# Gradient stores of a decode attention block: each 1.5 MB dV and dK tile stored in two halves

## The chip, the cores and the metric

The kernel runs on one core of a Trainium2 chip. The time is the device time of one execution, in microseconds. Each version is timed in several runs; one further execution is recorded by the profiler, and all durations by line, engine or stretch come from that one. Engines are named as in the profile: PE multiplies matrices, PEld loads its weights, DVE works on whole tiles elementwise, ACT does copies and functions, POOL and SP here do hardly more than start DMA transfers. The core has 16 DMA engines, which all queues share.

## What is computed

A block with a modulated layernorm, attention over a cache for one token, and an MLP, and then its gradients. The part that matters here is the attention and the gradients of its caches:

```python
B, Sq, D = (1, 1, 640)
Hq, Hkv, Sk, Dh = (32, 32, 8192, 192)
...
scores = jnp.einsum('bhqd,bhkd->bhqk', q, k) * Dh ** (-0.5)
p = _softmax(scores, axis=-1)
o = jnp.einsum('bhqk,bhkd->bhqd', p, v)
...
_out, _vjp = jax.vjp(_f, A_x, A_k_cache, A_v_cache, A_wq, A_wo, B_w3, B_w4, c, w_mod)
_grads = _vjp(grad_out)
```

K and V are 32 heads of 8192 x 192 in bf16, 3.1 MB each per head. Both are read, V twice (for the output and again for dP = dO V), and dK and dV of the same size are written. With p the softmax row of a head, dV is the outer product of p and dO, and dK the outer product of dS = p (dP - c) and q.

## The kernel before

**Two stages.** The first, up to about 560 us, goes through the heads with loads of K and V and computes the output. Then come a short seam, which does the MLP and its gradients, and the second stage, lines 1420 to 1507, which computes dK, dV and the gradients of the weights. It is a loop over 64 steps `s`; a step is one half `t` of the cache rows of one head (4096 rows), in the order of `ht(s)`, from the last head to the first. The order on PE, DVE, ACT and SP is the order in the program; POOL's DMAs go out in program order too.

**The layout.** A tile of a step has 128 partitions of 32 rows of 192 values: 12288 bytes per partition, 1.5 MB (1536 KB) in all. Row `j` of partition `p` lies beside row `j + 1` in memory, so a whole tile is a run of 12288 bytes for each partition. `JH` is 32 rows, a tile; `JQ` is 16 rows, half a tile.

**A step.** `dot_sum` and line 1427 turn the dot products of V and dO into `dS4`. Then these are woven into each other:
- `dv(0)` to `dv(7)` (lines 1113 to 1123) make dV in eight groups: four matmuls into PSUM (line 1122) and one ACT copy into the tile (line 1123) each. `gs` says which group comes when. An even group number writes rows 0 to 15 of every partition, the first half of the tile, an odd one rows 16 to 31.
- `dk_part` (line 1127) makes dK on DVE in two halves, `0:JQ` and `JQ:JH`.
- `tree_q` (line 1111), `mul_q` (line 1092) and `half_q` compute the dot products of the next steps, in halves too.
- `slot()` puts in a share of the side work: transposes and sums for the weights' gradients, their loads through SP, and their stores of 0.48 or 0.96 MB through POOL (lines 1217 and 1244).
- `load_v` asks SP for the V tile of step s + 5 once its buffer is free.

**The stores.** `dv_store` (line 1377) and `dk_store` (line 1381) take a range of rows. `dv_store` goes through POOL unless another queue is given. For most steps there is one `dk_store` of the whole tile after the second `dk_part`, and one `dv_store` of the whole tile after `dv(7)`. Exceptions: at step 0, dV was made before the loop and dK is stored in halves; at step 63 both are stored in halves, dV through SP, with `gs` in the order 0, 2, 4, 6, 1, 3, 5, 7.

**The buffers.** `OL` gives dV and dK of a step one of five tiles in turn (`OB`, named KB, VB and `qs_bc` in the profile). So dK of step s is written where dV of step s - 2 was, and dV of step s where dK of step s - 3 was; the new write waits until the store of those rows has landed. A wait concerns the rows that are written. V tiles have four other buffers, which come free when both `mul_q` of a step are done.

**POOL's DMA semaphores.** The framework gives the DMAs that POOL starts eight semaphores in turn. Ahead of each of these DMAs stands a semaphore instruction on POOL, which waits for the landing of the DMA eight before it on POOL; the wait for the data follows with the DMA itself.

Of the kernel before, what the change touches and what calls it, by code (L numbers as in the profile page):

```python
# [20 lines left out]
def kernel(  # L21
# [26 lines left out]
    nc = tc.nc  # L48
# [7 lines left out]
    JH = J // 2  # L56
    JQ = J // 4
# [59 lines left out]
    def tcol(n, name, dtype=FP32):  # L117
        return tmp.tile([P, n], dtype, name=name)
# [208 lines left out]
    def load_v(h, t, v):  # L327
        nc.sync.dma_start(out=v, in_=V_hd[h][:, t * JH : (t + 1) * JH, :])
        return v
# [16 lines left out]
    def dot_sum(ps, dst):  # L346
        V_.reduce_sum(out=dst, in_=ps, axis=AX.X)  # L347
# [11 lines left out]
    NS = 2 * HQ  # L359

    def load_er(s, eng=nc.scalar, er=None):

        if er is None:
            er = bst.tile([P, R8, P], BF16, name="er_b", bufs=2)
        h, t = ht(s)
        r0 = h * J + t * JH
        eng.dma_start(out=er[0:P:32, :, :].rearrange("r k p -> r (k p)"), in_=eT_d[r0 : r0 + JH, :].rearrange("(r k) p -> r (k p)", r=4))
        return er

    def ht(s):  # L370

        return H1 - s // 2, (1 - s % 2 if s < 2 else s % 2)
# [668 lines left out]
    def do_of(h):  # L1041
        return do_r[:, (TL - h // 2) % NDR, (h % 2) * DH : (h % 2 + 1) * DH]
# [24 lines left out]
    def q_bc(h, pool=psB, tag="b"):  # L1067
        ps = pool.tile([P, 2 * P], FP32, name="q_ps", tag=tag)
        T_.matmul(ps[:, 0:DH], lhsT=pick(HQ, h), rhs=q_rows, start=True, stop=True)
        qh = bst.tile([P, DH], BF16, name="qh", bufs=2)  # L1070
        A_.copy(out=qh, in_=ps[:, 0:DH])
        return qh
# [18 lines left out]
    def mul_q(s, q):  # L1091
        V_.tensor_tensor(  # L1092
            out=pq[:, q],
            in0=v_l[s][:, q * JQ : (q + 1) * JQ, :],
            in1=do_of(ht(s)[0])[:, None, :].to_broadcast([P, JQ, DH]),
            op=ALU.mult,
        )
# [4 lines left out]
    def half_q(s, q):  # L1102
        if halved(s, q):
            V_.tensor_tensor(out=pq[:, q, :, 0:HW], in0=pq[:, q, :, 0:HW], in1=pq[:, q, :, HW:DH], op=ALU.add)

    def tree_q(ps, s, q, lo=0, hi=DH // TS):
        w = DH
        if halved(s, q):
            w, lo, hi = HW, (lo + 1) // 2, (hi + 1) // 2
        for k in range(lo * TS, hi * TS, TS):  # L1110
            T_.matmul(ps[:, q * JQ : (q + 1) * JQ, :], lhsT=ident_bf, rhs=pq[:, q, :, k : k + TS], start=(k == 0), stop=(k == w - TS), skip_group_check=True)  # L1111

    def dv_groups(dV, er, doh, gs):

        dV4 = dV.rearrange("p (r k) d -> p r (k d)", r=4)
        for g in gs:
            m, q = divmod(g, 2)
            ps = psV.tile([P, 2, 512], FP32, name="dv_ps", tag="v")
            for k in range(2):
                for b in range(2):  # L1120
                    p0 = 32 * (2 * q + b)
                    T_.matmul(ps[:, b, k * DH : (k + 1) * DH], lhsT=er[p0 : p0 + 1, 2 * m + k, :], rhs=doh[p0 : p0 + 1, :], start=True, stop=True)  # L1122
            A_.copy(out=dV4[:, 2 * q : 2 * q + 2, m * PW : (m + 1) * PW], in_=ps[:, :, 0:PW])  # L1123

    def dk_part(dK, qh, dS4, lo, hi):
        n = hi - lo
        V_.tensor_tensor(  # L1127
            out=dK[:, lo:hi, :].rearrange("p j (a b) -> p j a b", b=4),
            in0=qh.rearrange("p (a b) -> p a b", b=4)[:, None, :, :].to_broadcast([P, n, DH // 4, 4]),
            in1=dS4[:, lo:hi, None, :].to_broadcast([P, n, DH // 4, 4]),  # L1130
            op=ALU.mult,
        )
# [207 lines left out]
    def slot():  # L1340
        prog[0] += 1
        k = prog[0] - 1
        due = sum(n for i, n in RAMP.items() if i <= k) if k < R0 else NR + -(-(NP - NR) * (k - R0 + 1) // (SLOTS - R0))
        while prog[1] < min(due, NP):
            next(side)
            prog[1] += 1

    def v_buf(s):
        return KY if s == 0 else VB[2] if s == 1 else (VB[0], VB[1], KX, KY)[(s - 2) % 4]
# [8 lines left out]
    def dq_rows(t, kb, dS4):  # L1358

        ps = psB.tile([P, 512], FP32, name="dq_ps", tag="b")  # L1360
        for j in range(JH):
            p0 = 32 * (j % 4)
            T_.matmul(ps[p0 : p0 + 32, 0:DH], lhsT=dS4[:, j, 0:1].to_broadcast([P, 32]), rhs=kb[:, j, :], start=(j < 4), stop=(j >= JH - 4), skip_group_check=True)
        row = bst.tile([P, DH], FP32, name="dq_junk")
        A_.copy(out=row, in_=ps[:, 0:DH])
        return row

    def dq_cols(row):
        cp = psS.tile([P, 4], FP32, name="dq_c", tag="s")
        T_.matmul(cp[:, 0:1], lhsT=row[:, 0:P], rhs=c32[:, 0:1], start=True, stop=True)  # L1370
        T_.matmul(cp[64:128, 1:2], lhsT=row[:, P:DH], rhs=c32[:, 0:1], start=True, stop=True)
        V_.tensor_tensor(out=dq_x[:, 2:3], in0=cp[:, 0:1], in1=dq_x[:, 2:3], op=ALU.add)
        V_.tensor_tensor(out=dq_x[64:128, 1:2], in0=cp[64:128, 1:2], in1=dq_x[64:128, 1:2], op=ALU.add)

    def dv_store(s, dV, lo, hi, eng=nc.gpsimd):
        h, t = ht(s)
        eng.dma_start(out=dV_hd[h][:, t * JH + lo : t * JH + hi, :], in_=dV[:, lo:hi, :])  # L1377

    def dk_store(s, dK, lo, hi):
        h, t = ht(s)  # L1380
        nc.gpsimd.dma_start(out=dK_hd[h][:, t * JH + lo : t * JH + hi, :], in_=dK[:, lo:hi, :])  # L1381
# [38 lines left out]
    for s in range(NS):  # L1420
        h, t = ht(s)
        nxt = s + 1 < NS
        doh = do_of(h)
        dP = tcol(JH, "dP")
        dot_sum(ps, dP)
        dS4 = bst.tile([P, JH, 4], BF16, name="dS4", bufs=2)
        V_.scalar_tensor_tensor(
            out=dS4,
            in0=dP[:, :, None].to_broadcast([P, JH, 4]),
            scalar=cpr[:, h : h + 1],  # L1430
            in1=E_all[:, h, t * JH : (t + 1) * JH, None].to_broadcast([P, JH, 4]),
            op0=ALU.subtract,
            op1=ALU.mult,
        )
        dV, dK = OL[2 * s], OL[2 * s + 1]
        gs = [0, 1, 2, 3, 4, 5, 6, 7]
        if not nxt:
            gs = [0, 2, 4, 6, 1, 3, 5, 7]
        if s == 0:
            gs = [None] * 8  # L1440
        else:
            er = er_l.pop(s)
        if nxt:
            ps = psR.tile([P, JH, TS], FP32, name="dot_ps")

        def dv(k):
            if gs[k] is not None:
                dv_groups(dV, er, doh, (gs[k],))

        def tree(q, lo, hi):  # L1450
            if nxt:
                tree_q(ps, s + 1, q, lo, hi)

        dv(0)
        dv(1)
        slot()
        tree(0, 0, 4)
        if nxt:
            mul_q(s + 1, 1)
            half_q(s + 1, 1)  # L1460
            v_l.pop(s + 1, None)
        if 0 < s < NS - 5:
            v_l[s + 5] = load_v(*ht(s + 5), v_buf(s + 5))
        dv(2)
        tree(0, 4, 8)
        dv(3)
        tree(0, 8, 12)
        dk_part(dK, qh, dS4, 0, JQ)
        if not nxt:
            dv_store(s, dV, 0, JQ, nc.sync)  # L1470
        if s in (0, NS - 1):
            dk_store(s, dK, 0, JQ)
        slot()
        dv(4)
        tree(1, 0, 3)
        dk_part(dK, qh, dS4, JQ, JH)
        if s > 0 and late0:
            late0.pop(0)()
        dk_store(s, dK, JQ if s in (0, NS - 1) else 0, JH)
        if row is not None:  # L1480
            dq_cols(row)
            row = None
        dv(5)
        tree(1, 3, 6)
        slot()
        dv(6)
        tree(1, 6, 9)
        dv(7)
        if s + 2 < NS:
            er_l[s + 2] = load_er(s + 2)  # L1490
        if s == 0:
            pass
        elif nxt:
            dv_store(s, dV, 0, JH)
        else:
            dv_store(s, dV, JQ, JH, nc.sync)
        tree(1, 9, 12)
        if h == H1:
            row = dq_rows(t, (KD, KE)[t], dS4)
        if s + 2 < NS:  # L1500
            assert (s + 2) // 4 in done
            mul_q(s + 2, 0)
            half_q(s + 2, 0)
        if nxt and ht(s + 1)[0] != h:
            qh = q_bc(ht(s + 1)[0])
        done_s[0] = s + 1
        slot()
# [33 lines left out]
```

## Time and profile before

| What | Value |
| --- | --- |
| Median of 3 runs | 1391.87 us (1390.95 to 1393.46) |
| The profiled execution's own time | 1394.3 us |
| Its span, first to last instruction | 1392.5 us |
| PE / DVE / ACT / POOL busy | 1181.5 / 1110.0 / 912.3 / 108.3 us |
| DMA packets and bytes | 76872, 569.38 MB, mean 409 GB/s |
| Of the packets, under 8 KB | 37182 |
| Whole dV and dK stores on POOL (1536 KB) | 74 + 25 + 25 |
| Halves on POOL (768 KB) from the dV and dK buffers | 4 + 2 |
| Halves on SP at step 63 | 2 |
| PE clock granted, from 640 us on | 0.50 to 0.57 |

All stretches are microseconds from the span's start. A line of the profile's groups names the line of the kernel, the engine, the operation and the tiles (written <- read). A wait line reads: engine, tile and line that waited, what released it, total us, times, the longest. A timeline row is start, duration, engine, line, operation, tiles, and in brackets the idle time of the engine before it with what ended it; a DMA row is the issue on the engine's queue, not the transfer. The DMA share of a stretch is the time of the packets that start in it over the time of 16 engines.

### The profile page before, as it was taken

The page shows a single profiled execution, that of the slowest core. Times are in us where ns is not written, and L with a number is a line of the kernel's source. Part 1 is how long each engine was busy: PE and PEld are TensorE (multiplying, and loading weights), DVE is VectorE, ACT ScalarE, POOL GpSimd, SP SyncE. Part 2 cuts the span into 40 slices and gives each one's busy share as a digit, 9 for nine tenths or more (in the row PEclk, how much of TensorE's full clock was granted, in tenths as well). Part 3 has the DMA queues.
Part 4 walks back from the last instruction along what each step waited for, and adds up shares of the span by engine and source line. Part 5 has one row for each costly group of instructions (what it writes and reads, how often), then busy time and mean ns, then how long its engine had stood idle before and what let it go on. Part 6 is the DMA issues. An engine that isn't in the chain of part 4 may idle for free.

```text
span 1392.5 us, 30504 instructions
## 1 busy us (share of the span) xinstructions
PE 1181.5 (85%) x12712; PEld 743.2 (53%) x12712; DVE 1110.0 (80%) x1455; ACT 912.3 (66%) x2007; POOL 108.3 (8%) x196
## 2 busy tenths in 40 slices
PE   3888999999899999988767998788989699779985
PEld 2777777778787778633323443334444344334431
DVE  4999999999999999986764875776766767768775
ACT  0677777777777778866554766665656566556664
POOL 0000000000000000111110110111110101101110
PEclk7899999999999999765555555665555555555555
DMA  9999999999999999699999999999999999999998
GB/s 381 390 404 422 413 424 424 410 417 420 418 420 419 408 418 387 231 419 427 423 397 401 428 424 427 423 425 425 426 418 425 421 409 427 420 409 384 423 412 353
DMA packets 76872, 569.38 MB, mean 409 GB/s; under 512 B 7422, under 2 KB 25198, under 8 KB 37182
## 3 DMA queue, kind: packets, MB, share of 16 engines
q1 hardware_dynamic: 51594, 342.03, 60.2%
q0 software_dynamic: 24624, 224.89, 38.5%
q8 instruction: 99, 1.62, 0.4%
q10 hardware_dynamic: 516, 0.51, 0.1%
q14 instruction: 39, 0.32, 0.1%
HBM read 340.97 MB, written 226.44 MB: 407 GB/s over the span
## 4 chain that ended last, share of the span: by engine, by line
issue 39%; DVE 23%; DMA 18%; PE 12%; POOL 4%; ACT 3%; POOLq 0%; SPq 0%; ACTq 0%; DVEq 0%
DMA KB<-in_A_k_cache_dram 10%; DVE prod L333 10%; DVE prod L337 5%; DVE vs L403 3%; DMA out_dram<-KB 3%; PE mp L425 2%; DMA out_dram<-VB 2%; PE dot_ps L1111 2%; PE half_ps L343 2%; POOL out_dram L1381 2%; DMA stg<-in_A_wq_dram 2%; POOL out_dram L1377 2%; PE mp L430 1%; DMA out_dram<-qs_bc 1%; PE dv_ps L1122 1%
## 5 line engine op out<-in xcount | busy, mean ns | idle before, releaser
L1111 PE MATMUL dot_ps<-pq,ident_bf 128*128 128x256 bf16 x1494 | 377.7, 396 | 21.7 <-DVE dP L347 19.8
L410 ACT ACTIVATE vs<-VB,Ef 128x192 bf16<-128x192 bf16 x840 | 303.6, 447 | 0.0
L1123 ACT CAST KB<-dv_ps 128x768 bf16<-128x768 f32 x312 | 241.4, 805 | 77.8 <-PE dv_ps L1122 76.5
L1111 PEld LDWEIGHTS <-ident_bf 128*128 128x128 bf16 x1494 | 149.9, 123 | 175.0 <-issue 136.2
L1122 PE MATMUL dv_ps<-do_r,er_b 1*128 1x192 bf16 x2016 | 226.8, 335 | 4.3 <-ACT KB L1123 3.1
L333 DVE TENSOR_TENSOR prod<-KB,qs_bc 128x6144 bf16<-128x6144 bf16 x62 | 207.9, 3353 | 25.4 <-DMA KB<-in_A_k_cache_dram 21.7
L425 PE MATMUL mp<-vs,KB 128*128 128x193 bf16 x1984 | 189.5, 247 | 4.4 <-ACT vs L410 3.3
L425 PEld LDWEIGHTS <-KB 128*128 128x128 bf16 x1984 | 168.9, 98 | 13.7 <-issue 7.6
L1127 DVE TENSOR_TENSOR KB<-qh,dS 128x3072 bf16<-128x3072 bf16 x74 | 127.7, 1752 | 54.8 <-DMA out_dram<-KB 40.7
L904 ACT COPY wT<-wT_ps 128x1024 bf16<-128x1024 bf16 x82 | 79.1, 965 | 119.3 <-PE wT_ps L903 119.2
L1122 PEld LDWEIGHTS <-er_b 1*128 1x128 bf16 x2016 | 69.3, 104 | 145.7 <-issue 143.8
L343 PE MATMUL half_ps<-prod,ident_bf 128*128 128x256 bf16 x744 | 95.1, 279 | 43.7 <-DVE prod L337 43.6
L403 DVE TENSOR_TENSOR vs<-VB,E 128x1728 bf16<-128x1728 bf16 x120 | 123.6, 1051 | 0.3 <-ACT vs L410 0.3
L1092 DVE TENSOR_TENSOR pq<-VB,do_r 128x3072 bf16<-128x3072 bf16 x66 | 115.4, 1749 | 9.7 <-PE dot_ps L1111 9.7
L1092 DVE TENSOR_TENSOR pq<-KB,do_r 128x3072 bf16<-128x3072 bf16 x62 | 108.4, 1749 | 6.4 <-PE dot_ps L1111 6.4
L337 DVE TENSOR_TENSOR prod<-prod 128x3072 bf16<-128x3072 bf16 x62 | 108.7, 1753 | 1.0
L343 PEld LDWEIGHTS <-ident_bf 128*128 128x128 bf16 x744 | 72.9, 100 | 62.2 <-issue 53.2
L430 PE MATMUL mp<-vs,KB 128*64 128x193 bf16 x1968 | 106.0, 250 | 0.0
L1123 ACT CAST VB<-dv_ps 128x768 bf16<-128x768 f32 x96 | 75.2, 803 | 39.7 <-PE dv_ps L1122 39.6
L347 DVE TENSOR_REDUCE dP<-dot_ps 128x32 f32<-128x512 f32 x64 | 44.0, 687 | 68.7 <-PE dot_ps L1111 68.5
L1123 ACT CAST qs_bc<-dv_ps 128x768 bf16<-128x768 f32 x104 | 79.9, 805 | 21.2 <-PE dv_ps L1122 20.8
L390 ACT ACTIVATE E<-S_h,negm 128x256 bf16<-128x256 f32 x31 | 15.8, 508 | 114.6 <-DVE negm L561 112.3
(377 smaller groups left out, 1256.8 us busy)
## 6 DMA issues: line engine op xcount, KB each, us to landing
VB<-in_A_v_cache_dram SPq DMA_DIRECT2D x93, 1536.0 KB
out_dram<-KB POOLq DMA_DIRECT2D x74, 1536.0 KB, 15.7
KB<-in_A_k_cache_dram SPq DMA_DIRECT2D x63, 1536.0 KB
KB<-in_A_v_cache_dram SPq DMA_DIRECT2D x29, 1536.0 KB
out_dram<-qs_bc POOLq DMA_DIRECT2D x25, 1536.0 KB, 15.2
out_dram<-VB POOLq DMA_DIRECT2D x25, 1536.0 KB, 15.0
wo_st<-in_A_wo_dram SPq DMA_DIRECT2D x31, 480.0 KB
w_st<-in_A_wq_dram SPq DMA_DIRECT2D x12, 960.0 KB
```

Of the source, the lines that this page charges most:

```text
L333: V_.tensor_tensor(out=prod, in0=src, in1=vec[:, None, :].to_broadcast([P, JH, DH]), op=ALU.mult)
L337: V_.tensor_tensor(out=prod[:, :, 0:HW], in0=prod[:, :, 0:HW], in1=prod[:, :, DH - HW : DH], op=ALU.add)
L343: T_.matmul(ps, lhsT=ident_bf, rhs=prod[:, :, k : k + TF], start=(k == 0), stop=(k == w - TF))
L403: V_.tensor_tensor(out=vs[:, 0:n, 0:DH].rearrange("p j (a b) -> p j a b", b=4), in0=v[:, v0 : v0 + n, :].rearrange("p j (a b) -> p j a b", ...
L410: A_.activation(out=vs[:, k, 0:DH], in_=v[:, v0 + k, :], func=ACT.Copy, scale=Ef[:, j0 + k : j0 + k + 1])
L425: T_.matmul(mp[:, 0:MW], lhsT=kb[:, j0 + k, 0:P], rhs=vs[:, k, 0:MW], start=(q == 0 and k == 0), stop=(z and k == JQ - 1), skip_group_chec ...
L430: T_.matmul(mp[p0 : p0 + 64, MO : MO + MW], lhsT=kb[:, j0 + k, P:DH], rhs=vs[:, k, 0:MW], start=False, stop=(z and k >= JQ - 2), skip_grou ...
L1092: V_.tensor_tensor(out=pq[:, q], in0=v_l[s][:, q * JQ : (q + 1) * JQ, :], in1=do_of(ht(s)[0])[:, None, :].to_broadcast([P, JQ, DH]), op=AL ...
L1111: T_.matmul(ps[:, q * JQ : (q + 1) * JQ, :], lhsT=ident_bf, rhs=pq[:, q, :, k : k + TS], start=(k == 0), stop=(k == w - TS), skip_group_ch ...
L1122: T_.matmul(ps[:, b, k * DH : (k + 1) * DH], lhsT=er[p0 : p0 + 1, 2 * m + k, :], rhs=doh[p0 : p0 + 1, :], start=True, stop=True)
L1123: A_.copy(out=dV4[:, 2 * q : 2 * q + 2, m * PW : (m + 1) * PW], in_=ps[:, :, 0:PW])
L1127: V_.tensor_tensor(out=dK[:, lo:hi, :].rearrange("p j (a b) -> p j a b", b=4), in0=qh.rearrange("p (a b) -> p a b", b=4)[:, None, :, :].to ...
```

## The change

All steps from 1 on make dV's first-half groups first, and store both dV and dK in two halves of 16 rows, 6144 bytes per partition. The first half of dV and the first half of dK are stored after the first `dk_part`, dV's ahead of dK's; the second half of dK after the second `dk_part`, the second half of dV after `dv(7)`. All go through POOL, but for step 63's dV, which goes through SP as before. Steps 0 and 63 store what they stored before.

```diff
         dV, dK = OL[2 * s], OL[2 * s + 1]
-        gs = [0, 1, 2, 3, 4, 5, 6, 7]
-        if not nxt:
-            gs = [0, 2, 4, 6, 1, 3, 5, 7]
+        gs = [0, 2, 4, 6, 1, 3, 5, 7]
         if s == 0:
             gs = [None] * 8
...
         dk_part(dK, qh, dS4, 0, JQ)
-        if not nxt:
-            dv_store(s, dV, 0, JQ, nc.sync)
-        if s in (0, NS - 1):
-            dk_store(s, dK, 0, JQ)
+        if s > 0:
+            dv_store(s, dV, 0, JQ, nc.gpsimd if nxt else nc.sync)
+        dk_store(s, dK, 0, JQ)
         slot()
...
         dk_part(dK, qh, dS4, JQ, JH)
         if s > 0 and late0:
             late0.pop(0)()
-        dk_store(s, dK, JQ if s in (0, NS - 1) else 0, JH)
+        dk_store(s, dK, JQ, JH)
...
-        if s == 0:
-            pass
-        elif nxt:
-            dv_store(s, dV, 0, JH)
-        else:
-            dv_store(s, dV, JQ, JH, nc.sync)
+        if s > 0:
+            dv_store(s, dV, JQ, JH, nc.gpsimd if nxt else nc.sync)
```

## The prediction, made before the changed kernel ran

> **What bounds the kernel now.** First the page's slices of DMA time and its table of queues.
>
> ```profile
> DMA  9999999999999999699999999999999999999998
> ...
> q1 hardware_dynamic: 51594, 342.03, 60.2%
> q0 software_dynamic: 24624, 224.89, 38.5%
> ```
>
> A digit is a fortieth of the span, 34.8 us. The 16 DMA engines are 90% busy or more in all but two: the seam between the two stages and the last slice. Loads (q1, issued by SP) take 60.2% of the engines' time and POOL's stores (q0) 38.5%, together 98.7%. Next the same by stretches; the columns are stretch, length, busy us with counts for PE, PEld, DVE, ACT and POOL, then granted clock, DMA share, GB/s.
>
> ```profile
> 900.00:1000.00 100.00, 85.31 (x622) 41.02 (x622) 72.85 (x109) 62.34 (x88) 11.26 (x20) 0.55 1.01 425
> ...
> 1353.00:1362.00 9.00, 7.23 (x48) 2.62 (x44) 8.93 (x8) 5.51 (x8) 1.06 (x2) 0.50 0.88 367
> 1362.00:1371.00 9.00, 7.61 (x51) 2.33 (x47) 8.90 (x9) 6.79 (x10) 1.06 (x2) 0.50 0.89 375
> 1371.00:1380.00 9.00, 6.72 (x50) 2.54 (x48) 7.35 (x6) 8.48 (x12) 2.12 (x4) 0.50 0.76 317
> ```
>
> In a plain stretch of the gradient stage the DMA share is 1.01, while PE is busy 85 us of 100, DVE 73, ACT 62: the DMA engines are the bound, and compute has room. The share can pass 1 because a packet counts in the stretch where it starts. Only after 1353 us, when the last load is in, does the share fall: there DVE (8.9 of 9 us) sets the pace. So the gradient stage obeys two prices: what the DMA engines do until about 1350 us, and when the last stores come to them after it.
>
> The waits of DVE between 620 and 1340 us show how the bound is felt: dK is written (line 1127) when the store that held its buffer has landed, 27 waits, 90.7 us.
>
> ```profile
> DVE KB L1127 <- DMA out_dram<-KB: 40.7, 13, 8.3
> DVE qs_bc L1127 <- DMA out_dram<-qs_bc: 31.7, 8, 6.8
> DVE VB L1127 <- DMA out_dram<-VB: 18.3, 6, 5.8
> ```
>
> **The change part by part.** *How many.* Steps 0 and 63 store in halves already, so steps 1 to 62 change: 62 dV and 62 dK, the 74 + 25 + 25 = 124 whole stores in the page's list of DMA issues. Each partition of a whole store is one packet of 12288 bytes; 128 become 256 of 6144. Each DMA also ends with one packet of a few bytes for each engine (in the stretches below, the packets under 512 bytes). So 124 x (128 + 16) = 17,856 packets more (76,872 to about 94,700), 1116 for each engine, with the same bytes.
>
> *The price of a packet.* Three stretches of the DMA view (packets, MB, share of 16 engines) differ in packet size. At 600 to 613 us nearly all are 12288 bytes:
>
> ```profile
> DMA packets 517, 5.63 MB, mean 433 GB/s; under 512 B 55, under 2 KB 55, under 8 KB 60
> ...
> q0 software_dynamic: 307, 3.34, 60.4%
> q1 hardware_dynamic: 201, 2.27, 41.0%
> ```
>
> At 1383.5 to 1389 us all data are the last step's halves, 6144 bytes:
>
> ```profile
> DMA packets 431, 2.35 MB, mean 428 GB/s; under 512 B 48, under 2 KB 48, under 8 KB 431
> ...
> q1 hardware_dynamic: 219, 1.25, 54.1%
> q0 software_dynamic: 212, 1.11, 48.2%
> ```
>
> And at 752.2 to 755.6 us the loads are weight rows of 1536 bytes:
>
> ```profile
> q1 hardware_dynamic: 563, 0.86, 67.8%
> ```
>
> Let a packet cost a, and a megabyte b, of one engine's time. First stretch, q1: 0.410 x 16 x 13 = 85.28 us = 201a + 2.27b, so b = 37.57 us - 88.5a. Second, both queues: 1.023 x 16 x 5.5 = 90.02 us = 431a + 2.35b, so 223a = 1.73 us, a = 7.8 ns. Third: 0.678 x 16 x 3.4 = 36.88 us = 563a + 0.86b, so 487a = 4.57 us, a = 9.4 ns. These are the two ends; I take the middle, 8.6 ns. Then 1116 x 8.6 ns = **9.6 us** more on each engine (8.7 to 10.5). Until 1350 us nothing hides it, as the share there is already 1.01; the five tail steps hold 10 of the 124 stores, 0.8 us of it.
>
> Here a rule stands against the change more heavily. The Trainium skill (DMA: Bandwidth & Descriptors, "Anatomy of one DMA — SWDGE (gpsimd) path") gives a DMA a fixed 2.0 us beside its bytes; paid in turn, 124 DMAs would be an estimated 248 us by that page, where the sum above has 9.6. It comes back as a rival.
>
> *POOL's issues.* A store's issue is 0.53 us on POOL, 124 more are 66 us, beside 108.3 us of 1392.5 now. The view of line 1377 (dV's stores):
>
> ```profile
> L1377 POOLq EVENT_SEMAPHORE  x65: 17/17/43, 568.8 to 1374.3; - x65
> L1377 POOL DMA_DIRECT2D out_dram<-KB x39: 532/532/582, 574.4 to 1374.8; - x39
> ...
> DMA to landing us min/median/max: 3.5/16.8/24.3
> ```
>
> A store lands a median 16.8 us after its issue, though 1.57 MB at 425 GB/s are 3.7 us: some 13 us of work queue ahead of it, which cover the 0.53 us. Cost: nothing.
>
> *The new waits.* The first-half dV store now stands on POOL ahead of the first-half dK store, and waits for ACT's fourth copy of line 1123; behind it queue the dK halves and the side work's stores, and for their landing wait DVE's next dK and SP's loads into the weight buffers. Each in program order, under the same 13 us: nothing. The semaphore instruction of 17 ns in the view is the wait for the DMA eight before, as POOL's DMAs use eight semaphores in turn. Now POOL issues 20 per 100 us and eight span 40 us; with about 16 more, eight span 22 us, and the slowest landing is 24.3 us. So this wait, free until now, will bind at times, by 24.3 - 22 = 2 us or so. By then seven stores of 0.77 MB, 12.7 us of DMA time, are queued: nothing again, and a rival below.
>
> *The order of dV's groups* puts two groups of the same rows behind one another. Step 63 already does so, and four of line 1122's matmuls take 0.50 us there as in step 62. Nothing.
>
> *What comes earlier.* In the DMA-bound part a store handed over earlier only queues longer. In the tail it is worth something; POOL's timeline:
>
> ```profile
> 1364.62 0.53 POOL L1381 DMA_DIRECT2D out_dram<-KB  x1 [7.60 <-DVE KB L1127]
> 1366.07 0.53 POOL L1377 DMA_DIRECT2D out_dram<-qs_bc  x1 [0.92 <-ACT qh L1071]
> 1374.27 0.53 POOL L1381 DMA_DIRECT2D out_dram<-VB  x1 [7.66 <-DVE VB L1127]
> 1374.79 0.53 POOL L1377 DMA_DIRECT2D out_dram<-KB  x1
> ```
>
> Step 62's 3.1 MB reach the queue only at 1374.3 to 1374.8, after a hole in the DMA (0.76 at 1371 to 1380), and with step 63's 3.1 MB they set the end: 6.3 MB at 425 GB/s are 14.8 us, 1389. With halves, its first dV half can go at about 1370.5 and its first dK half at 1372.3 (DVE began that write at 1370.55, 1.75 us each half): 1.57 MB, 3.7 us of DMA time, move into the hole. The holes after 1353 sum to 9 x (0.12 + 0.11 + 0.24) = 4.2 us, the most there is to gain; at the least nothing. I take **3.5 us**, near the 3.7.
>
> Sum: 9.6 - 3.5 = +6.1 us; the profiled execution (1394.3 us, span 1392.5) would take 1400.4, span 1398.6. It lies 2.4 us above the median of the runs, 1391.87, which becomes **1398.0**.
>
> **The rivals.** *No gain in the tail* (chance 0.15): POOL's order, or DVE late by what it waits for, leaves the hole. Then +9.6: 1401.5. Against it: the halves of step 63 went out within 0.4 us of their writes.
>
> *Nothing to tell* (0.15; within 0.2%, 2.8 us, about what a measurement of this kernel can tell from no change): the lower packet price, 8.7, less the tail's whole 4.2, and 2 us regained as under the next: +2.5, 1394.4.
>
> *Faster* (0.10), the other side. The second dK half waits as long as now, but the first finds its half free earlier; DVE then spends less of its 90.7 us in waits, compute runs further ahead, V buffers come free sooner and the DMA engines lose their poor stretches. Their rates per 100 us from 700 on are 408, 425, 425, 422, 419 and 403 GB/s; all at 425 would save 4.0 + 0.7 + 1.4 + 5.2 = 11.3 us. With the tail's 4.2: 9.6 - 15.5 = -5.9, 1386.0. It decides once 8.2 of the 11.3 are regained (9.6 - 4.2 + 2.8). Against it: the share is 1.00 to 1.01 in those stretches too, and two of them are poor for the 1536-byte loads that they hold, which stay.
>
> *The eight semaphores* (0.05): POOL held 2 us in each of 62 steps, a twentieth of it felt by the DMA engines: 6 us more, 1404. For it: the bursts of stores in a step are uneven; against it the 12.7 us queued.
>
> *Each DMA pays its landing by itself* (0.01): the two 768 KB stores alone at the end landed in a median 4.2 us, 1.85 us of it data at 425 GB/s; 2.35 x 124 = 291 us, 1683. That is the rule named above; the stretch at 1383.5 speaks against it, where halves follow one another with the engines' share at 1.02.
>
> **How the numbers follow.** The sum as worked out has 0.54, with its own range 1395 to 1401 (packet price 8.7 to 10.5, tail 2 to 4.2). Slower by over 0.2%: 0.54 + 0.15 + 0.05 + 0.01 = 0.75; within 0.2%: 0.15; faster: 0.10. The range reaches down to 1392, most of the no-change case, and up to 1403 past the case without a tail gain; left out are faster, the slots, the fixed cost and the lower edge of no change, some 0.2.
>
> **What would show it.** Packets near 94,700 with the same megabytes; between 650 and 1340 us a DMA share still of 1.00 to 1.01, and GB/s lower by 1.2% in stretches of like loads (9.6 of 790 us); the two stores of a step on POOL as four; the semaphore instruction of line 1377 longer than 17 ns at its longest, without a hole in the DMA; step 62's first halves issued some 3 us ahead of its second, and the share after 1371 near 1. DVE's waits at line 1127 for landings may shrink; if they do and the span doesn't, the DMA engines were the bound. The forecast is wrong if the share before 1340 falls under 0.99 (a new wait), or if the stage's bytes take no longer (packets free).

## The result and the profile after

The changed kernel takes 1395.81 us (median of 22 runs), the kernel before, run beside it, 1393.70 (22 runs): ratio 1.0021, 95% interval 1.0012 to 1.0030, so 2.9 us slower (1.7 to 4.2). The forecast was +6.1 and a time of 1398.0; the time lies in the stated range of 1392 to 1403, the difference is about half of the one forecast.

The two profiled executions both span 1392.5 us, which looks like no change at all. They have to be read by stages. The last dS of the loop (line 1427) starts at 1374.6 us before and 1373.8 after, but the first at 575.7 and 571.3: the first stage, which the change doesn't touch, happened to be 4.4 us shorter in the second recording. From the first dS to the end it is 816.8 us before and 821.2 after. One recording of each kernel stands behind such figures, and recordings of like kernels differ by several us, as a kernel below shows whose time is that of before.

The page's counts after the change:

```profile
DMA packets 94730, 569.41 MB, mean 409 GB/s; under 512 B 9406, under 2 KB 27182, under 8 KB 70910
...
q1 hardware_dynamic: 51594, 342.03, 59.7%
q0 software_dynamic: 42480, 224.90, 39.1%
```

17,858 packets more, the same bytes. The stores' packets took 0.6% of the engines' time more, 8.4 us, a little under the 9.6 priced; the loads' took 0.5% less, though not one of them was changed. The stretches (busy us by engine, clock, DMA share, GB/s):

```profile
900.00:1000.00 100.00, 92.81 (x640) 44.62 (x638) 72.36 (x108) 64.27 (x89) 19.02 (x35) 0.50 1.02 421
...
1353.00:1362.00 9.00, 8.56 (x54) 3.10 (x54) 8.93 (x9) 6.56 (x9) 2.20 (x5) 0.50 0.87 354
1362.00:1371.00 9.00, 7.61 (x50) 2.51 (x50) 8.90 (x8) 6.71 (x10) 2.13 (x4) 0.50 0.87 357
1371.00:1380.00 9.00, 5.93 (x44) 2.31 (x43) 6.57 (x6) 7.98 (x11) 2.65 (x5) 0.50 0.99 408
```

The share is now 1.02 in the plain stretch, and the hole after 1371 us is closed (0.76 before). DVE's waits from 620 to 1340 us for a landing:

```profile
DVE KB L1127 <- DMA out_dram<-KB: 79.8, 27, 6.6
DVE qs_bc L1127 <- DMA out_dram<-qs_bc: 47.0, 12, 9.1
DVE VB L1127 <- DMA out_dram<-VB: 45.3, 12, 9.1
```

51 waits and 172.1 us, where there were 27 and 90.7. A first half no longer has to wait for a whole store, yet stores of half the size land later than the whole ones did, as the view of line 1377 says in its last line (16.8 us the median before):

```profile
L1377 POOLq EVENT_SEMAPHORE  x127: 17/17/43, 564.4 to 1373.5; - x127
...
  DMA out_dram<-KB: 19.5, 8
  DMA out_dram<-qs_bc: 14.7, 7
...
DMA to landing us min/median/max: 3.5/19.6/28.2
```

The two lines in the middle are POOL's idle time before these stores that a landing ended: the wait for the DMA eight before. It is there now, 46 times and 106 us over all of POOL's lines, and it shows as idle time, not as a longer semaphore instruction. POOL's last steps:

```profile
1370.04 0.53 POOL L1377 DMA_DIRECT2D out_dram<-KB  x1 [4.21 <-ACT KB L1123]
1371.82 0.53 POOL L1381 DMA_DIRECT2D out_dram<-VB  x1 [1.25 <-DVE VB L1127]
1373.49 0.53 POOL L1381 DMA_DIRECT2D out_dram<-VB  x1 [1.14 <-DVE VB L1127]
1374.01 0.53 POOL L1377 DMA_DIRECT2D out_dram<-KB  x1
```

Step 62's first halves go out at 1370.0 and 1371.8, as foretold; the end did not come earlier by it.

### The profile page after: what moved, and what is told of

It is laid out like the page before. It is cut to its first block, busy times and chain, and to the rows that moved or that the text cites. A ratio compares the mean times of both kernels' runs of the same rounds, so it can differ in the third digit from the quotient of the medians.

```text
span 1392.5 us, 30826 instructions
## 1 busy us (share of the span) xinstructions
PE 1198.6 (86%) x12712; PEld 755.9 (54%) x12712; DVE 1109.7 (80%) x1455; ACT 915.3 (66%) x2007; POOL 174.6 (13%) x320
## 4 chain that ended last, share of the span: by engine, by line
DMA 51%; DVE 23%; PE 14%; issue 8%; ACT 2%; POOL 1%; SPq 0%; ACTq 0%; POOLq 0%; DVEq 0%
DMA out_dram<-KB 12%; DMA KB<-in_A_k_cache_dram 10%; DMA out_dram<-VB 10%; DMA out_dram<-qs_bc 9%; DVE prod L333 9%; DVE prod L337 5%; PE dot_ps L1111 3%; DVE vs L403 3%; PE mp L425 3%; DMA out_dram<-wo_st 2%; DMA w_st<-in_A_wq_dram 2%; PE half_ps L343 2%; PE dv_ps L1122 2%; DMA out_dram<-w_st 1%; PE mp L430 1%
## 5 line engine op out<-in xcount | busy, mean ns | idle before, releaser
L1111 PE MATMUL dot_ps<-pq,ident_bf 128*128 128x256 bf16 x1494 | 384.3, 401 | 42.3 <-DVE dP L347 42.1
L1122 PE MATMUL dv_ps<-do_r,er_b 1*128 1x192 bf16 x2016 | 239.1, 342 | 3.6 <-ACT KB L1123 2.9
L1122 PEld LDWEIGHTS <-er_b 1*128 1x128 bf16 x2016 | 80.2, 108 | 147.6 <-issue 145.9
L390 ACT ACTIVATE E<-S_h,negm 128x256 bf16<-128x256 f32 x31 | 15.7, 508 | 115.4 <-DVE negm L561 113.1
L430 PEld LDWEIGHTS <-KB 128*64 128x64 bf16 x1968 | 78.8, 109 | 19.8 <-issue 19.4
```

The source lines that it names most:

```text
L430: T_.matmul(mp[p0 : p0 + 64, MO : MO + MW], lhsT=kb[:, j0 + k, P:DH], rhs=vs[:, k, 0:MW], start=False, stop=(z and k >= JQ - 2), skip_grou ...
```

## The experiments

Twelve kernels ran. Each time stands as its ratio to the kernel before, run on the same chip, with its 95% interval; microseconds are the ratio times 1393.7. The diffs are against the kernel before.

**Late halves.** The price of the packets alone:

```diff
-        dk_store(s, dK, JQ if s in (0, NS - 1) else 0, JH)
+        if late:                      # late = 0 < s < NS - 1
+            dk_store(s, dK, 0, JQ)
+        dk_store(s, dK, JQ if s in (0, NS - 1) or late else 0, JH)
...
-            dv_store(s, dV, 0, JH)
+            if late:
+                dv_store(s, dV, 0, JQ)
+            dv_store(s, dV, JQ if late else 0, JH)
```

> All of steps 1 to 62 store both tiles in two halves, but both halves only where the whole store stood, with the old order of dV's groups: the price of the 17,856 more packets alone, nothing earlier. The prediction's theory (a packet's fixed time is paid in full on its engine): +9.6 us on the kernel before, ratio 1.0069. The rival from the changed kernel's profile (packets of the two queues overlap on an engine, so that the price by bytes per wall time is 5.5 ns): +6.1 us, 1.0044. If packets are free: within 2 us of before, and the changed kernel's few us come from elsewhere.

Measured: 1.0002 (0.9990 to 1.0014), +0.3 us, at most +2.0. The prediction's +9.6 is excluded, and so is the 6.1 of the overlap alone. In this kernel 124 more DMAs and 17,856 more packets cost next to nothing on balance.

**Early halves in the tail alone**, in steps 59 to 62, and **in the body alone**, in steps 1 to 58:

```diff
-        if not nxt:
+        if not nxt or early:          # early = NS - 5 <= s < NS - 1, or 0 < s < NS - 5
             gs = [0, 2, 4, 6, 1, 3, 5, 7]
...
+        elif early:
+            dv_store(s, dV, 0, JQ)
-        if s in (0, NS - 1):
+        if s in (0, NS - 1) or early:
             dk_store(s, dK, 0, JQ)
...
```

The stores of the second halves, left out here, change as in the diff before.

> Halves stored early, and dV's first-half groups first, in steps 59 to 62 alone, after the last load is asked for; all else as before. The prediction's theory: 8 more DMAs cost 0.6 us and the hole in the tail gives 3.5, so -2.9 us, 0.9979. The rival: DVE sets the pace of the tail and the DMA engines end soon after it anyway; the tail gives under 1 us, ratio 0.9995 to 1.0005.

Measured: 1.0006 (0.9990 to 1.0022), +0.8 us; a gain of 2.9 is excluded.

> Halves stored early, and dV's first-half groups first, in steps 1 to 58 alone, the tail with whole stores as before. The prediction's theory: 116 more DMAs, +9.0 us, 1.0065, as the DMA engines are full and earlier stores only queue. The rival (early halves keep the store queue filled, loads run less alone, and a part of the poor stretches is regained): +1 to +4 us, and clearly below the run with late halves.

Measured: 1.0009 (0.9997 to 1.0020), +1.3 us. That is far from +9.0, but not below the late halves either, so the rival's second half is not confirmed.

**The order of dV's groups alone:**

```diff
-        if not nxt:
+        if not nxt or s > 0:
             gs = [0, 2, 4, 6, 1, 3, 5, 7]
```

> Only the order of dV's groups is changed (first-half groups first at every step), all stores whole as before. Both theories: no change, ratio 0.999 to 1.001. If it is slower by 0.2% or more, the order is part of the changed kernel's loss.

Measured: 0.9993 (0.9977 to 1.0009): no change that can be told. Its one recording still took 823.4 us from the first dS to the end, 6.6 more than the recording of before. That is how far a single recording can stray, here with an execution of 1397.97 us in a kernel whose median is 1394.01.

**The DMA engines by themselves.** Four kernels do nothing but these transfers:

```python
for s in range(2 * HQ):
    ...
    if LOADS:
        nc.sync.dma_start(out=LB[s % 4], in_=V_hd[h][:, t * JH : (t + 1) * JH, :])
    for k, hd in ((0, dV_hd), (1, dK_hd)):
        ...
        for a in range(PARTS):
            ...
            nc.gpsimd.dma_start(out=hd[h][:, t * JH + lo : t * JH + hi, :], in_=o[:, lo:hi, :])
```

> DMA alone: the 128 stores of dV and dK (201 MB) from five unchanging tiles through POOL, whole, 12288-byte packets; no loads and no computation, all other outputs left out. 201.3 MB at 427 GB/s: 471 us and some 10 us around it. Base for the next run.

> The same stores in two halves each, 6144-byte packets, 128 more DMAs and 18,432 more packets, 1152 for each engine. The prediction's price (8.6 ns) gives +9.9 us on the whole stores; the interval between packets that follow one another on a single engine in the changed kernel's tail (230.6 ns for 6144 bytes, 456 for 12288, so 5 ns) gives +5.8 us; free packets give under 1 us.

Measured: 495.6 us whole (4 runs, 495.5 to 495.7) and 515.6 in halves (515.4 to 515.6): +20.0 us, twice the highest expectation. For 1152 packets on each engine that is 17.4 ns a packet. The base was slower than expected too: some 481 us had been reckoned at 427 GB/s, and 418 were moved.

> DMA alone with both queues: the 128 whole stores beside 64 loads of V of 1.5 MB through SP into four tiles, as in the gradient stage; no computation, other outputs left out. 302 MB at 427 GB/s: 707 us. Base for the next run. SP's loads wait for the load four before.

> The same with the stores in halves. The prediction's price: +9.9 us; 5 ns: +5.8 us; if a packet's fixed time hides under the other queue's data where both queues have work: clearly less than the two runs without loads differ by, down to nothing.

Measured: 716.7 and 738.9 us (4 runs each, all within 0.3 us of these): +22.3, more than without loads and more than any of the three expectations. The sum hides two regimes. In both kernels the loads are done first, beside stores, and then stores go on alone; with halves the loads are done sooner, so that more of the stores are left to go alone. The stretches of the kernel with whole stores and loads, then of the one with halves (length, busy DVE and POOL, clock, DMA share, GB/s):

```profile
40.00:340.00 300.00, 0.00 (x0) 21.85 (x41) 1.00 1.01 430
530.00:690.00 160.00, 0.00 (x0) 21.86 (x41) 1.00 1.01 419
```

```profile
40.00:340.00 300.00, 0.00 (x0) 28.78 (x54) 1.00 1.01 428
530.00:690.00 160.00, 0.00 (x0) 43.17 (x81) 1.00 1.01 402
```

Beside loads, halving the stores costs 2 GB/s of 430; alone it costs 17 of 419. The two queues in the first of these stretches (packets, MB, share), whole stores and then halves:

```profile
q1 hardware_dynamic: 5906, 64.51, 50.4%
q0 software_dynamic: 5904, 64.49, 50.4%
```

```profile
q1 hardware_dynamic: 7840, 85.72, 67.0%
q0 software_dynamic: 7839, 42.76, 34.1%
```

This is the reading that explains most of the rest. The engines take the two queues' packets by turns, one for one. (The records don't name a packet's engine, but a packet starts a few ns before the end of the one ahead of it on its engine. Where only one such packet can be found, from 100 to 140 us, it is of the other queue in 1028 of 1028 cases with whole stores and in 1140 of 1141 with halves.) With packets of one size the bytes are shared half and half; with the stores' packets halved, the loads get two thirds. The Trainium skill (DMA: Bandwidth & Descriptors, "Queues, rings and completion order") says that an engine goes round its queues at the granularity of packets, and counts a packet as some 9 to 17 descriptors; the turns agree with the counts of 7840 and 7839, but here a turn is a single piece of 6144 or 12288 bytes. From the bytes (128.48 MB against 129.00 in 300 us, and half of the 7839 packets, 3920, there only because of the halving) a packet beside loads costs 1.2 us x 16 / 3920, about 5 ns.

**The loads in halves**, first with the stores as before, then with the change: the shares tilted the other way, and level again.

```diff
-            v_l[s + 5] = load_v(*ht(s + 5), v_buf(s + 5))
+            v_l[s + 5] = v_buf(s + 5)
+            load_v5(JQ, JH, s + 5)
+            load_v5(0, JQ, s + 5)
```

> The stores as before; each V load from step 6's on in two DMAs of 6144 bytes per partition at the place of the whole one, second half first, so that neither is asked for earlier. Theory now (an engine takes the packets of the two queues by turns, one for one, so the queue with the smaller packets gets fewer bytes): where both have work the loads fall to a third of the bytes; the stores are ahead at the end, and from the last load's landing to the end of the DMAs it takes 45 to 49 us instead of 51; but the stores' queue runs dry more often, so loads alone take more of the stage than the kernel before's 38 us. Time: within 3 us of before, either way. Rival (packets cost by their number alone): +2.7 us, and neither shift.

Measured: 1.0042 (1.0026 to 1.0059), +5.9 us, more than the 3 us allowed either way, and more than the rival's 2.7. Both shifts came: from the last load to the last packet some 44 us, against 51 before, even less than the 45 to 49 expected, and 46 us of loads alone. What wasn't foreseen is the price. The side work's weights come through the same queue as V, and PE now waits longer for them; PE's waits from 620 to 1340 us:

```profile
PE wT_ps L903 <- DMA wo_st<-in_A_wo_dram: 37.2, 6, 14.9
PE wT_ps L903 <- DMA stg<-in_A_wq_dram: 21.9, 2, 12.4
PE wT_ps L903 <- DMA w_st<-in_A_wq_dram: 18.6, 3, 12.0
PE wT_ps L903 <- DMA w_st<-in_w_mod_dram: 6.6, 2, 4.5
```

These are 84.3 us. The same four lines add up to 55.6 in the kernel before and, without the last, which is missing there, to 16.1 in the changed kernel, whose loads get the larger share. That these waits are what costs the 5.9 us fits, but no run changes them alone.

> The change as it is, and the V loads in halves as in the run beside it: packets of one size on both queues again. Theory now: the shares of bytes go back to those of before; from the last load's landing to the end 51 to 52 us instead of the changed kernel's 55, and more time with loads alone than its 5 us. Time: the changed kernel's or 1 to 3 us less, so ratio 1.000 to 1.002. Rival (number of packets): +2.7 us on the changed kernel, 1.004.

Measured: 1.0017 (1.0003 to 1.0031), +2.4 us, within what was expected of the time. The loads alone rose only from 5 to 9 us, and the last packet came some 54 us after the last load, against 55 in the changed kernel and not 51 to 52, for a reason that the next section shows.

**By stage**, the attempt at something better than both (late halves in steps 1 to 44; V loads asked for from step 47 on in halves):

> An attempt at a version that beats both: stores in halves at the place of the whole one in steps 1 to 44, whole from there; V loads asked for from step 47 on in halves. Theory now: the first part keeps the stores' queue from running dry (38 to under 15 us of loads alone in that part), the second puts the stores ahead, so that the end comes 47 to 50 us after the last load. Together -2 to -5 us, ratio 0.9965 to 0.9985. If the mixture of the packets does not matter: 0 to +2 us.

Measured: 1.0058 (1.0036 to 1.0081), +8.1 us. One step, the 52nd, took 28 us: PE waited 16.0 us in it for one load of weights (`w_st`). The end of the span came 47.4 us after the last load (the last packet 45.6), about as expected, but the load itself came at 1353.2 us instead of 1339.2.

**dK's halves alone:**

```diff
-        if s in (0, NS - 1):
+        if s in (0, NS - 1) or early:      # early = 0 < s < NS - 1
             dk_store(s, dK, 0, JQ)
...
-        dk_store(s, dK, JQ if s in (0, NS - 1) else 0, JH)
+        dk_store(s, dK, JQ if s in (0, NS - 1) or early else 0, JH)
```

> Half of the change: dK alone stored in two halves as they are made (steps 1 to 62), dV whole and its groups in the old order. 62 more DMAs, 28 per 100 us, so that eight of them span some 28 us and POOL hardly waits for the landing of the one eight before. If what the changed kernel loses beside the run with late halves comes from those waits or from dV's early halves: within 1 us of before, 0.9995 to 1.0007. If it comes with each early half alike: +1.2 to 1.5 us, 1.001. The prediction's prices would give +4.8 less 1.7 in the tail, 1.0022.

Measured: 1.0002 (0.9988 to 1.0016), +0.3 us. POOL waited for the DMA eight before once, 2.7 us. It is the first of the cases expected, but the interval (-1.7 to +2.2 us) doesn't exclude the second.

## Why the prediction came out as it did

The direction was right, and so was the bound: from 600 to 1340 us the DMA share stays at 1.00 to 1.02. The mechanism was not: the packets, which were to cost 9.6 us, cost 0.3 on balance where they were changed alone, and the tail, which was to give 3.5, gave nothing that can be told. That these two errors partly cancelled, and that the time came to lie in the range, is luck. Where the 2.9 us come from is only in part known. Five points of the profiled executions, in us from the span's start, worked out from the trace's packets and line 1427, show how ("most engines" is when fewer than half of the 16 are still at work, "last packet" the last of loads and stores):

| | first dS | last load landed | last dS | most engines done | last packet | span |
| --- | --- | --- | --- | --- | --- | --- |
| before | 575.7 | 1339.2 | 1374.6 | 1390.3 | 1390.4 | 1392.5 |
| changed | 571.3 | 1334.1 | 1373.8 | 1386.3 | 1389.4 | 1392.5 |
| late halves | 571.3 | 1334.3 | 1372.8 | 1387.0 | 1388.8 | 1391.9 |
| tail alone | 573.8 | 1338.1 | 1375.6 | 1388.1 | 1390.6 | 1393.1 |
| body alone | 572.8 | 1334.2 | 1373.9 | 1389.6 | 1389.7 | 1392.3 |
| order alone | 572.8 | 1341.7 | 1378.3 | 1394.0 | 1394.1 | 1396.2 |
| dK's halves alone | 573.3 | 1336.0 | 1373.0 | 1387.2 | 1387.9 | 1392.1 |
| loads halved | 576.2 | 1354.9 | 1382.7 | 1398.4 | 1398.5 | 1400.7 |
| both halved | 574.1 | 1338.4 | 1375.7 | 1388.1 | 1392.3 | 1395.3 |

**"The price of a packet"** is the step that failed most. It came to 9.6 us on the path; measured, the packets alone cost 0.3 us on balance (-1.4 to 2.0). Two things were wrong in it. First, the sum of the packets' durations was taken for the engine's time. It isn't: a share of 1.01 or 1.02 over 100 us can't come from a packet counted in the wrong stretch, as the prediction said of it, but from packets that overlap. On the one engine that works alone at the end of the changed kernel, most packets of 234 ns start 230 to 231 ns apart. The price beside loads is 5 ns, not 8.6, and alone 17.4; for 1116 packets on each engine these are 5.6 to 19.4 us. Second, "until 1350 us nothing hides it" left out that the part had slack. From the first dS to the last load it is 763.5 us before and 762.8 after, with more packets and the same bytes: the prediction had named that itself as a sign of being wrong ("if the stage's bytes take no longer"). The recording of the order alone, at 768.9, warns against reading tenths here, but the late halves (763.0) and the body alone (761.4) say the same. What paid for them are stretches in which loads run alone at a poor rate; before, at 714 to 720 us:

```profile
DMA packets 166, 1.82 MB, mean 303 GB/s; under 512 B 16, under 2 KB 16, under 8 KB 20
...
q1 hardware_dynamic: 125, 1.54, 85.9%
q0 software_dynamic: 41, 0.28, 16.8%
```

The DMA share is above 1 there, and only 303 GB/s move. The 100 us around it, before and after:

```profile
700.00:800.00 100.00, 77.70 (x574) 37.23 (x574) 66.61 (x96) 58.63 (x83) 11.25 (x20) 0.57 1.01 408
```

```profile
700.00:800.00 100.00, 94.57 (x641) 44.43 (x641) 69.42 (x98) 65.58 (x90) 19.26 (x35) 0.50 1.02 422
```

From 1200 to 1300 us it is 403 and 413 GB/s, while plain stretches fall, the one from 900 from 425 to 421. Counted in microseconds of which 90% or more of the bytes were loads, these are 38 us of the stage before, at 366 GB/s, 5 us after, 6 with late halves, 4 with the body alone. With a third of the bytes instead of half, the stores' queue no longer runs dry. Against 425 GB/s that is a loss of 5.3 us before and 0.8 after; the order alone and the tail alone, whose body stores whole tiles, have 4.1 each. In all other microseconds, counted the same way from 580 us on, the loss rose from 8.4 us to 11.5. These 3.1 us are less than the 4.5 regained, and less than the 5.6 that 5 ns a packet would give; but the order alone, with whole stores, has 14.6 here, so no packet price can be read from it. Why the 17.4 ns of the stores alone don't show in this kernel, where 226 us carry 90% or more of stores, is open. So a full DMA share was not a full DMA engine. The prediction had this as its rival of regained poor stretches and gave it 0.10 and, in part, 0.15; the way it came, through the turns of the two queues rather than through DVE's shorter waits, it had not. That the regained stretches cancel the packets' price is worked out from these counts of one recording each; no run has the one without the other.

**"What comes earlier"**, -3.5 us, came out at +0.8 (-1.4 to 3.1) in the run with the tail alone. The hole did close, and the time from the last dS until most engines are done fell from 15.7 us to 12.5, 3.2, near the 3.5 reckoned. But then one engine goes on. The changed kernel's end:

```profile
1380.00:1386.40 6.40, 0.00 (x0) 0.00 (x0) 0.00 (x0) 0.00 (x0) 0.00 (x0) 0.50 0.99 411
1386.60:1389.40 2.80, 0.00 (x0) 0.00 (x0) 0.00 (x0) 0.00 (x0) 0.00 (x0) 0.50 0.06 26
```

A share of 0.06 is one sixteenth: one of the 16 engines is behind the others by some 3 us, and the last store lands when it is done. So it is 15.8 us from the last dS to the last packet before and 15.6 after: of the 3.2 us 0.2 are left. Another 1.0 us is lost behind the last packet, where no DMA moves any more: the span goes on for 2.1 us before and 3.1 after. In the trace a last instruction of POOL, a DRAIN, ends 1.0 us after the last landing before and 1.9 after, and in the kernels of DMA alone 0.95 with whole stores and 1.84 with halves. Over all runs it is 0.7 to 3.0; what sets it is open. The kernel before has no engine left alone at its end:

```profile
1371.00:1374.40 3.40, 3.21 (x24) 1.02 (x24) 3.40 (x3) 2.92 (x5) 0.14 (x1) 0.50 0.62 260
1374.40:1375.20 0.80, 0.60 (x6) 0.35 (x7) 0.73 (x3) 0.80 (x2) 0.80 (x2) 0.50 0.00 0
1380.00:1390.00 10.00, 0.00 (x0) 0.00 (x0) 0.00 (x0) 0.00 (x0) 0.00 (x0) 0.50 1.01 423
```

At 1374.4 all its engines are out of work for 0.8 us. By the trace's packets most of them had run dry at 1373.2 and the last one at 1374.4: the hole was where late engines caught up. (That it is the same engine at both places isn't shown, as the records don't name engines.) All three kernels of the table with early halves of dV and dK in steps 59 to 62 show the lone engine, for 2.5 to 4.2 us, the late halves for 1.8, dK's halves alone for 0.7; with whole stores at the end it is 0.1. "Both halved" missed its mark by this. The hole's mean share was read as time that all 16 engines could use; for the engine that ends last it was 0.8 us.

**What no term had**: from the last load to the last dS it takes 35.4 us before and 39.7 after (38.5 late, 39.7 body alone, 36.6 order alone, 27.8 with the loads halved). The megabytes left when the last load lands are nearly the same, 19.70 and 19.77:

```profile
1339.20:1392.50 53.30, 34.91 (x220) 12.45 (x220) 37.60 (x32) 30.63 (x42) 5.63 (x11) 0.50 0.88 370
```

```profile
1334.10:1392.50 58.40, 36.04 (x229) 13.44 (x229) 42.59 (x45) 30.90 (x42) 12.12 (x22) 0.50 0.82 339
```

DVE has 42.6 us of work left there instead of 37.6: the loads, with the larger share, finish earlier than the computation can follow, which waits for stores to land (DVE from 1300 to 1380 us: 5.2 us before, 13.9 after), and after the last load DVE sets the pace. The share falls to 0.82. This account is argued from the traces; no run tests it by itself. The profiled pair adds up to -0.7 us to the last load, +4.3 to the last dS, +0.8 to the end of the span, +4.4 in all, against 1.7 to 4.2 by the times.

**The other points.** POOL's issues (as many in the late halves, at +0.3 us) and the order of dV's groups cost nothing that can be told, as said. The eight semaphores bind, 2.3 us each time as reckoned (2 us), without a hole in the body's DMA share. Whether they cost something is open: the changed kernel (46 waits, 106 us) is at +2.9 us, the body alone (44, 107 us) at +1.3, late halves (21, 40 us) and dK alone (1, 2.7 us) at +0.3. The order fits, but all the intervals overlap, the changed kernel's and the late halves' by a sliver (1.0012 and up, 1.0014 and down). So handing over early may cost some 2.6 us beside handing over late; neither that nor its cause is settled. The rival that each DMA pays its landing by itself is refuted: 128 more DMAs cost 20.0 us where stores run alone, 0.16 us each, and the fixed 2.0 us of the Trainium skill (DMA: Bandwidth & Descriptors, "Anatomy of one DMA — SWDGE (gpsimd) path") is not paid by DMAs that queue.

No version beat the kernel before; the nearest, late halves and dK's halves alone, can't be told from it.

## What to carry to other kernels

Where two DMA queues competed here, the size of their packets set how they shared the engines: halving one side's packets handed bytes to the other, and what waited for the slower side was late. So look for the side that paces a kernel before resizing either. A DMA share of 1 says that packets are in flight, not that bytes move at the full rate: compare GB/s in like stretches, and don't build on a few us between two single recordings. A hole in the tail may be one in which the slowest engine catches up; before counting it as gain, see for how long the share falls to nothing in it.

## What was not expected of the hardware

The cost of packets of 6144 instead of 12288 bytes depends on what runs beside them: 428 against 430 GB/s beside loads, 403 against 418 over 420 us of stores alone. Packets of one engine overlap by a few ns, so that shares of 1.02 are real. And one engine of 16 was 2 to 4 us behind the others at the end of a long saturated stretch.
